# Decode attention with adaptive layernorm and token MLP: four stages as wide matmuls, and the last head with V as the stationary operand

## The chip, the cores and the metric

One core of one Trainium2 chip. The metric is the time of one execution of the whole program on the device, in microseconds; the profile's span is counted from the first to the last instruction of one profiled execution.

## The reference

One decode step of a transformer block, four batches (B), one token each, model width D = 512, everything in fp32. Six vectors of modulation come from `silu(c) @ w_mod`. Attention has 32 query heads of width 128 that share 8 K/V heads (four query heads each) over a cache of 4096 positions. The second half is the token-mixing MLP of an MLP-Mixer with a token axis of length 1: each of the 512 channels is expanded to 1792 values, passed through Gelu and contracted to one value again.

```python
mod = (silu(c) @ w_mod).reshape(B, 6, 1, -1)          # sa, ca, ga, sb, cb, gb
h = layernorm(x) * (1 + ca) + sa
q = (h @ wq).reshape(B, 1, 32, 128) ...
p = softmax(q @ k.T * 128 ** -0.5)                      # per head, k and v shared by 4 heads
x = x + ga * ((p @ v) @ wo)
h = layernorm(x) * (1 + cb) + sb
u = gelu(layernorm(h)[b, 0, d] * w1[0, f] + b1[f])      # (B, D, F), F = 1792
x = x + gb * (u @ w2 + b2)
```

## The kernel before

The work is a list of 32 heads (4 batches x 8 K/V heads; `i = b * 8 + h`). Each head brings a K tile and a V tile, 2 MB each, which go through one ring of five buffers of that size (`ring`, tag `kv`); the weights of the query projection and of the modulation use the same ring. All loads are issued on SyncE's queue in program order: in pass `i` of the main loop (L446) K of head `i + 3` and V of head `i + 1`. A K buffer comes free when the scores of its head are done, a V buffer when its values are done. The last V is cut into pieces of a half, a quarter and two eighths (L177).

The order of the instructions on every engine is the order of the program (`manual_schedule`, L42). Pass `i` holds, in this order:

- an epilogue step, if `i % 8 == 5` (L450);
- `transposes(i + 1)` (L231): eight 128x128 transposes of the exponentials `p`, the row sums `pl`, then on VectorE (DVE) the copy `pT`, the reciprocal and `sel`, which selects and scales the rows of a query head;
- `project_a(i - 1)` (L266): one matmul with the values `po` as stationary operand and `sel` as moving one, which gives the head's output transposed, `oT`;
- `scores(i + 2)` (L200): eight matmuls of 512 columns, with the four query heads in 32-column strips of the array, so that a strip `c` (partitions 32c to 32c + 31 of the result) holds a quarter of the positions; then the maximum `m` of each row;
- `project_b(i - 1)` (L274): 16 matmuls of 128 columns against `wo`, each strip `c` holding a quarter of the 512 channels, all four query heads accumulated in PSUM; then the add onto the batch's accumulator on DVE;
- `colmax(i + 2)` and `expo(i + 2)` (L211, L219): the maximum over the four strips (a transpose and a DVE reduction `mx` of 128 elements), its broadcast `pb` by four matmuls, and the exponential on ScalarE (ACT);
- an epilogue step of the batch before, if `i % 8 < 5` (L467);
- in passes 3 to 5 one modulation vector (`mod`, L193), which is computed for each batch separately, 64 matmuls in all;
- `values(i)` (L248): 32 matmuls of 128 columns. Block `k` of the positions and strip `c` choose the stationary piece of `pT` and the moving 128 positions of V; each strip accumulates over eight blocks. Then `po`, the copy out of PSUM, on DVE (L259).

PE is TensorE; an fp32 matmul appears in the profile as two, each with its own weight load (PEld).

A batch's second half runs as a generator, `epilogue` (L362), whose steps are handed out one per pass: in pass `i % 8 == 0` statistics, in 1 the layernorm, in 2 the second layernorm, the broadcast of the channels to all partitions and the first three Gelus of 1024 elements a partition (L379), in 3 the contraction of those (`contract`, L356) and two more Gelus, in 4 the same with the last two, in 5 the last contraction. For batch 2 half of this last contraction waits until the end (L386, L486). Gelu and exp need different activation tables on ACT.

For the last batch the gate `ga` is folded into `wo` of head 7 beforehand (`fold_gate`, L429, in pass 25), so that the last projection accumulates straight onto the residual in PSUM (`pgx`, L484). After the loop come `project_a`, `project_b` of head 30, the values of head 31 and its projection (L480 to L488), and `finish` (L391): the whole epilogue of batch 3 with nothing beside it but the last modulation vector (the gate `gb`), then two output DMAs.

In the kernel before, `px`, `prep`, the accumulator and everything of a batch in the second half have 128 columns with strip `c` holding channels 128c to 128c + 127, 32 equal rows in each strip.

## Time and profile before

| | |
|---|---|
| median of the runs | 396.02 us (395.72 to 396.19) |
| span of the profiled execution | 394.4 us, some 1.6 us less than the time of a run |
| TensorE | busy 73% of the span, 5414 matmuls and as many weight loads |
| DVE, ACT | busy 38% and 24% |
| DMA | 158 MB, mean 401 GB/s |
| granted TensorE clock, mean | 0.943 |

A line of a timeline gives the start and the length in us, the engine, the line of the kernel, the operation, what is written from what, the shapes, the number of instructions merged in the line, and in brackets the idle time of the engine before it with what ended it. A group's line has the busy time in us and the mean of one in ns, then the idle time before and its releasers. A window's line has, after its length, the busy time and the count on PE, PEld, DVE, ACT and POOL, then the granted clock, the share of the DMA engines and GB/s. PEld is the part of TensorE that loads the stationary operand. Matmuls are pipelined, so the mean of one is longer than the distance between two. A few records of matmuls are missing in the trace, which shows as short idle times put down to "issue".

### The profile page before, as it was taken

To read this page: it belongs to the slowest core of one execution; us is meant where nothing else is said; L and a number is where in the kernel's file an instruction comes from. 1 tells how busy PE (TensorE), PEld (TensorE's weight loads), DVE (VectorE), ACT (ScalarE), POOL (GpSimd) and SP (SyncE) were. 2 spreads that over 40 slices of the span, in tenths; PEclk is the share of its full clock that TensorE was granted. 3 is DMA by queue.
4 is the path that set the end of the run, shared out by engine and by line. 5 is a ranking of instruction groups with operands and counts; after the bars stand their busy time and mean duration, and the time that the engine had idled before them with its cause. 6 is when DMAs were issued, how large, how long until landed. Compare 5 with 4: busy or idle time off the path is not lost.

```text
span 394.4 us, 11762 instructions
## 1 busy us (share of the span) xinstructions
PE 288.9 (73%) x5414; PEld 194.4 (49%) x5414; DVE 151.4 (38%) x487; ACT 96.4 (24%) x119; POOL 0.7 (0%) x6
## 2 busy tenths in 40 slices
PE   0976785539967586778677787779776787897884
PEld 0122444408745444556455455557544464675763
DVE  4222222203222232556432334546323345763266
ACT  1001111101110111136641011348411010685125
POOL 0000000000000000000000000000000000000000
PEclk9989689959999889999999899989999898999999
DMA  8999999999999999999999999999999999999700
GB/s 321 425 430 437 431 419 433 420 430 433 429 420 432 429 429 429 427 432 429 429 421 429 430 434 429 424 425 431 432 429 427 425 429 434 427 425 417 289 8 2
DMA packets 12720, 158.08 MB, mean 401 GB/s; under 512 B 1516, under 2 KB 1532, under 8 KB 1920
## 3 DMA queue, kind: packets, MB, share of 16 engines
q1 hardware_dynamic: 12672, 157.34, 93.9%
q8 instruction: 42, 0.69, 0.6%
q14 instruction: 6, 0.05, 0.0%
HBM read 157.32 MB, written 0.01 MB: 399 GB/s over the span
## 4 chain that ended last, share of the span: by engine, by line
DMA 56%; PE 29%; DVE 8%; ACT 4%; issue 1%; SPq 0%; ACTq 0%; DVEq 0%
DMA k<-in_kT 43%; DMA v<-in_v 11%; PE s L205 10%; PE pv L254 5%; DVE m L208 3%; PE s L126 2%; PE s L235 2%; DMA sm<-in_small 2%; PE py L359 2%; DVE u L354 1%; PE pa L282 1%; ACT uu L414 1%; PE pm L190 1%; ACT p L228 1%; PE qs L141 1%
## 5 line engine op out<-in xcount | busy, mean ns | idle before, releaser
L205 PE MATMUL s<-k,QT 128*32 128x512 f32 x512 | 74.0, 703 | 40.3 <-DMA k<-in_kT 40.2
L228 ACT ACTIVATE p<-s,nm 128x1024 f32<-128x1024 f32 x32 | 35.6, 1114 | 234.5 <-DVE nm L225 234.5
L208 DVE TENSOR_REDUCE m<-s 128x1 f32<-128x1024 f32 x32 | 39.2, 1225 | 101.5 <-PE s L205 101.5
L254 PE MATMUL pv<-v,pT 128*32 128x128 f32 x2048 | 64.5, 277 | 5.6 <-DMA v<-in_v 4.5
L254 PEld LDWEIGHTS pv<-v,pT 128*32 128x32 f32 x2048 | 56.2, 111 | 7.6 <-DMA v<-in_v 5.3
L205 PEld LDWEIGHTS s<-k,QT 128*32 128x32 f32 x512 | 14.7, 119 | 66.4 <-DMA k<-in_kT 41.4
L282 PEld LDWEIGHTS pa<-wo,oT 128*32 128x32 f32 x992 | 30.2, 116 | 22.3 <-issue 21.2
L235 PE MATMUL s<-ident,p 128*128 128x128 f32 x256 | 36.4, 286 | 0.7 <-ACT p L228 0.4
L282 PE MATMUL pa<-wo,oT 128*32 128x128 f32 x992 | 34.6, 282 | 0.8 <-DVE oT L271 0.8
L235 PEld LDWEIGHTS s<-ident,p 128*128 128x128 f32 x256 | 28.6, 145 | 6.9 <-issue 6.3
L259 DVE COPY po<-pv 128x128 f32<-128x128 f32 x32 | 9.3, 290 | 41.9 <-PE pv L254 41.9
L354 DVE TENSOR_SCALAR u<-hb,wr,sm 128x512 f32<-128x512 f32 x42 | 20.0, 542 | 2.5 <-PE py L359 2.2
L214 PE MATMUL pm<-ident,m 128*1 128x128 f32 x32 | 8.7, 271 | 16.7 <-DVE m L208 16.7
L379 ACT ACTIVATE u<-u 128x1024 f32<-128x1024 f32 x21 | 20.9, 1047 | 0.1
L238 DVE COPY pT<-s 128x128 f32<-128x128 f32 x32 | 9.3, 290 | 24.8 <-PE s L235 23.6
L223 PE MATMUL pb<-neg,mx 1*32 1x1 f32 x256 | 7.6, 176 | 13.3 <-DVE mx L216 13.3
L214 PEld LDWEIGHTS pm<-ident,m 128*1 128x1 f32 x32 | 2.5, 79 | 28.8 <-DVE m L208 28.8
L126 PE MATMUL s<-wm,sT 128*4 128x512 f32 x16 | 9.6, 771 | 9.7 <-DVE sT L114 9.7
L269 PE MATMUL pt<-sel,po 128*128 128x4 f32 x64 | 11.8, 254 | 4.5 <-DVE po L259 2.9
L228 ACT ACT_TABLE_LOAD x9 | 11.5, 1283 | 13.2 <-DVE nm L225 13.1
L223 PEld LDWEIGHTS pb<-neg,mx 1*32 1x32 f32 x256 | 4.9, 103 | 19.5 <-DVE mx L216 19.5
L359 PE MATMUL py<-u,sm 128*32 128x128 f32 x336 | 11.6, 276 | 2.9 <-ACT u L379 2.9
(114 smaller groups left out, 233.1 us busy)
## 6 DMA issues: line engine op xcount, KB each, us to landing
k<-in_kT SPq DMA_DIRECT2D x32, 2048.0 KB, 22.6
v<-in_v SPq DMA_DIRECT2D x29, 2048.0 KB, 22.5
wq<-in_wq SPq DMA_DIRECT2D x4, 2048.0 KB, 18.0
wo<-in_wo SPq DMA_DIRECT2D x8, 1024.0 KB, 23.1
v<-in_v SPq DMA_DIRECT2D x5, 1024.0 KB, 19.0
wm<-in_wmod SPq DMA_DIRECT2D x2, 2048.0 KB
wm<-in_wmod SPq DMA_DIRECT2D x2, 1024.0 KB, 16.4
v<-in_v SPq DMA_DIRECT2D x1, 512.0 KB, 20.2
```

Of the source, the lines that this page charges most:

```text
L126: mm(s0[0:B, t * D:(t + 1) * D], sT[:, k, :], wm01[:, t, k, :], start=(k == 0), stop=(k == 3))
L205: mm(s[32 * c:32 * c + 32, n * 512:(n + 1) * 512], QT[:, b, h, :], KT[i][:, (n * 4 + c) * 512:(n * 4 + c + 1) * 512], start=True, stop=True)
L208: dv.tensor_reduce(m, s, axis=AX.X, op=OP.max)
L223: mm(pb[32 * c:32 * c + 32, :], mx, neg1, start=True, stop=True)
L228: nc.scalar.activation(p, s, AF.Exp, bias=nm, accum_out=l)
L235: nc.tensor.transpose(pt[:, k, :], p[:, k * P:(k + 1) * P], ident)
L254: mm(pv[32 * c:32 * c + 32, :], pTs[i % 2][:, k, c, :], VT[i][:, k * 4 + c, :], start=(k == 0), stop=(k == 7))
L269: mm(pt, po, sel, start=True, stop=True)
L282: mm(pa[32 * c:32 * c + 32, :], oT[:, g:g + 1].to_broadcast([P, 32]), wo_t[h][:, g, c * P:(c + 1) * P], start=(g == 0 and not folded), sto ...
L354: dv.tensor_scalar(u[:, e, :], hb, wr[:, j:j + 1], b1[:, j:j + 1], op0=OP.mult, op1=OP.add)
L359: mm(py[32 * c:32 * c + 32, :], w2[:, j:j + 1].to_broadcast([P, 32]), u[:, e, c * P:(c + 1) * P], start=(j == 0), stop=(j == NF - 1))
L379: nc.scalar.activation(u, u, AF.Gelu_apprx_tanh)
```

## The change

- *Values.* Eight matmuls of 512 columns instead of 32 of 128: all 16 used columns of a block (four strips of four query heads) against four neighbouring pieces of V at once. A strip now holds two of the eight blocks, and of the 16 x 512 results in it only the matching quarters are wanted. The copy `po` is four times as wide and moves from DVE to ACT.
- *Project_a.* Four matmuls, accumulated, each with a 128x128 piece of `po` as stationary operand; `sel` (16 columns) picks the wanted quarter.
- *Project_b.* Four matmuls of 512 columns, strip `g` holding query head `g`; the accumulator is 128x512. The four rows are summed once for a batch (`fold_groups`) by four matmuls, before the residual.
- *Modulation and `px`.* All four batches at once: the 32 columns of a strip are four batches of eight rows (`sT8`, `rows`). So `prep` has no batch axis; the rows of batch `b` start at `32 c + 8 b`.
- *Contraction of batches 0 to 2.* Column block `j` of the MLP goes whole (512 columns) into strip `j % 4`; a copy `yw` and `fold_groups` follow. The step in which the last blocks are contracted is pass `i % 8 == 5`, for batch 2 too, and one more step follows in pass 6. The contraction of batch 3 stays narrow.
- *Maximum.* `mx` is written four times over by one reduction that reads its input four times, and `pb` is one matmul.
- *The last batch.* The gate is folded into `wo` of heads 6 and 7 (passes 25 and 26); heads 30 and 31 are projected straight onto the residual. Head 31 has V as the stationary operand: 32 matmuls of four columns, whose result is the transposed output, scaled in one multiply; no `po` and no `project_a`.
- *Output.* One DMA for each batch, that of batch 2 on ACT's queue, instead of one for batches 0 to 2 and one for batch 3.

```diff
-    def modmm(pm, t, steps):
-        for b, k in steps:
+    def modmm(pm, t):
+        for k in range(4):
             for c in range(4):
-                mm(pm[32 * c:32 * c + 32, b, :], sT[:, k, b:b + 1].to_broadcast([P, 32]),
+                mm(pm[32 * c:32 * c + 32, :], sT8[:, k].rearrange("p b r -> p (b r)"),
                    WM[t][:, k, c * P:(c + 1) * P], start=(k == 0), stop=(k == 3))
...
-        dv.tensor_reduce(mx, pm.rearrange("o (c r) -> o r c", c=4), axis=AX.X, op=OP.max)
+        dv.tensor_reduce(mx, pm.rearrange("o (c r) -> o r c", c=4).unsqueeze(1).to_broadcast([1, 4, 32, 4]),
+                         axis=AX.X, op=OP.max)
...
-        for c in range(4):
-            mm(pb[32 * c:32 * c + 32, :], mx, neg1, start=True, stop=True)
+        mm(pb, mx.rearrange("o c r -> o (c r)"), neg1, start=True, stop=True)
...
+    def values(i):
+        pv = ps_v.tile([P, 4 * DH], F32, name="pv")
+        for k in range(8):
+            q = k % 4
+            mm(pv[32 * q:32 * q + 32, :], pTs[i % 2][:, k, :],
+               VT[i][:, k * 4:(k + 1) * 4, :].rearrange("p j d -> p (j d)"), start=(k < 4), stop=(k >= 4))
+        po = wk.tile([P, 4 * DH], F32, name="po")
+        nc.scalar.activation(po, pv, AF.Copy)
+        SP[i] = (SEL.pop(i), po)
...
+    def values_last(i, js):
+        if js[0] == 0:
+            PV[i] = ps_v.tile([P, REP], F32, name="pvT", tag="pv")
+        for j in js:
+            k, c = divmod(j, 4)
+            mm(PV[i], VT[i][:, j, :], pTs[i % 2][:, k, c * REP:(c + 1) * REP], start=(j == 0), stop=(j == 31))
+        if js[-1] == 31:
+            oT = wk.tile([P, REP], F32, name="oT")
+            dv.tensor_mul(oT, PV.pop(i), SEL.pop(i))
+            OT[i] = oT
...
-        mm(pt, po, sel, start=True, stop=True)
+        for c in range(4):
+            mm(pt, po[:, c * DH:(c + 1) * DH], sel[:, c * REP:(c + 1) * REP], start=(c == 0), stop=(c == 3))
...
+        pa = ps_m.tile([P, D], F32, name="pa", tag="m")
+        for g in range(REP):
+            mm(pa[32 * g:32 * g + 32, :], oT[:, g:g + 1].to_broadcast([P, 32]), wo_t[h][:, g, :],
+               start=True, stop=True)
+        if h == 0:
+            ACC[b] = wk.tile([P, D], F32, name="acc")
+            dv.tensor_copy(ACC[b], pa)
+        else:
+            dv.tensor_add(ACC[b], ACC[b], pa)
...
+    def fold_groups(pool, acc, tag):
+        pc = pool.tile([P, P], F32, name="pc", tag=tag)
+        for c in range(4):
+            mm(pc[32 * c:32 * c + 32, :], first, acc[:, c * P:(c + 1) * P], start=True, stop=True)
+        return pc
...
+    def contract_wide(py, u, js):
+        for e, j in enumerate(js):
+            q = j % 4
+            mm(py[32 * q:32 * q + 32, :], w2[:, j:j + 1].to_broadcast([P, 32]), u[:, e, :],
+               start=(j < 4), stop=(j >= NF - 4))
...
         for u, js in done:
-            contract(py, u, js)
-            if b == B - 2:
-                yield
-        dv.tensor_scalar(ZK[:, b], py, b2, None, op0=OP.add)
+            contract_wide(py, u, js)
+        yw = wk.tile([P, D], F32, name="yw", bufs=1)
+        dv.tensor_copy(yw, py)
+        yield
+        dv.tensor_scalar(ZK[:, b], fold_groups(ps_e, yw, "e"), b2, None, op0=OP.add)
         yield
...
-        if i % HKV == 5:
+        if i % HKV >= 5:
             next(epi, None)
...
-        values(i, range(8))
-        if i == NS - HKV + 1:
-            fold_gate()
+        values(i)
+        if NS - HKV < i <= NS - HKV + 2:
+            fold_gate(HKV - 3 + i - (NS - HKV))
+    residual(ep, fold_groups(ps_e, ACC.pop(B - 1), "e"))
+    pgx = ps_s.tile([P, 8, P], F32, name="pgx", tag="s")
+    x3 = pgx[:, 4]
     project_a(NS - 2)
-    project_b(NS - 2)
-    values(NS - 1, (0, 1, 2, 3, 4, 5))
-    pgx = ps_s.tile([P, 8, P], F32, name="pgx", tag="s")
-    mm(pgx[:, 4], ident, EP.pop(B - 1), start=True, stop=False)
-    values(NS - 1, (6, 7))
-    next(epi)
-    project_a(NS - 1)
-    project_b(NS - 1, pgx[:, 4])
-    finish(B - 1, pgx, pgx[:, 4], epi)
+    mm(x3, ident, ep, start=True, stop=False)
+    project_direct(NS - 2, x3, False)
+    values_last(NS - 1, range(0, 28))
+    values_last(NS - 1, range(28, 32))
+    project_direct(NS - 1, x3, True)
+    finish(B - 1, pgx[:, 0], x3, epi)
```

`project_direct` issues the 16 narrow matmuls that `project_b` issued before, onto `x3`.

More of the change, by code (lines that the diff above doesn't have):

```diff
@@ L335, in bcast @@
         for c in range(4):
-            mm(pb[:, c, :], ident[:, 32 * c:32 * c + 1].to_broadcast([P, P]), h1, start=True, stop=True)
+            e = 32 * c + 8 * b
+            mm(pb[:, c, :], ident[:, e:e + 1].to_broadcast([P, P]), h1, start=True, stop=True)
         return pb.rearrange("p c n -> p (c n)")
@@ L393, in finish @@
         U = [uu[j // 8][:, j % 8] for j in range(NF)]
-        stm = stats(xp)
+        stm = stats(xp, b)
         dv.tensor_copy(XK[:, b], xp)
-        gate = [divmod(e, 4) for e in range(4 * B)]
         pst = gather(stm)
-        modmm(pg, 5, gate[:6])
+        modmm(pg, 5)
         h1, stm = adaln(b, pst)
@@ L445, in adaln_decode @@
     epi = iter(())
+    ep = cst.tile([P, P], F32, name="ep")
     for i in range(NS - 1):
```

143 lines of the change are left out of this document (62 added, 81 removed).

## The prediction

> **What bounds the kernel now.** I read the slices of the span first, then the busy time by windows, then the groups of instructions, and last the timeline of one ordinary pass of the main loop, of the three passes in which the token MLP of batch 2 is worked off, and of the end.
>
> ```profile
> DMA  8999999999999999999999999999999999999700
> ```
> ```profile
> 200.00:240.00 40.00, 30.41 (x556) 20.40 (x558) 13.24 (x46) 5.28 (x9) 0.00 (x0) 0.96 1.01 428
> 374.50:375.00 0.50, 0.50 (x23) 0.50 (x27) 0.00 (x0) 0.00 (x0) 0.00 (x0) 1.00 0.60 229
> ```
>
> The transfers fill the span up to about 375 us. One pass brings one K and one V, 4.194 MB, which at 428 GB/s is 9.80 us: a pass whose instructions take less waits for DMA, a pass that takes more falls behind, and the passes after it may catch up. What is behind when the last V has landed is paid in full, and so is everything after it. The question is therefore what the change does to the length of a pass, and to the end.
>
> **The wide matmuls.** Groups of instructions (count, busy us, mean ns of one):
>
> ```profile
> L205 PE MATMUL s<-k,QT 128*32 128x512 f32 x512 | 74.0, 703 | 40.3 <-DMA k<-in_kT 40.2
> L254 PE MATMUL pv<-v,pT 128*32 128x128 f32 x2048 | 64.5, 277 | 5.6 <-DMA v<-in_v 4.5 <-issue 0.9
> L208 DVE TENSOR_REDUCE m<-s 128x1 f32<-128x1024 f32 x32 | 39.2, 1225 | 101.5 <-PE s L205 101.5
> L216 DVE TENSOR_REDUCE mx<-pm 1x32 f32<-1x128 f32 x32 | 8.9, 277 | 4.6 <-PE pm L214 4.6
> L290 DVE TENSOR_TENSOR acc<-acc,pa 128x128 f32<-128x128 f32 x24 | 6.7, 279 | 3.2 <-PE pa L282 3.2
> L435 DVE TENSOR_TENSOR wo<-wo,pgb 128x512 f32<-128x512 f32 x4 | 2.5, 682 | 0.3 <-PE pgb L432 0.3
> L347 ACT ACTIVATE hb<-phb,nmean 128x512 f32<-128x512 f32 x3 | 2.1, 687 | 0.5 <-PE phb L336 0.2
> ```
>
> And an ordinary pass in order of time (start us, us), the last two lines from another pass:
>
> ```profile
> 314.31 1.95 PE L254 MATMUL pv<-v,pT 128*32 128x128 f32 x64
> 316.20 0.86 PEld L235 LDWEIGHTS s<-ident,p 128*128 128x128 f32 x8 [0.20 <-issue]
> 317.02 0.30 PEld L237 LDWEIGHTS pl<-l,grp 128*128 128x128 f32 x2
> 317.24 0.30 PEld L269 LDWEIGHTS pt<-sel,po 128*128 128x128 f32 x2
> 318.17 1.92 PE L205 MATMUL s<-k,QT 128*32 128x512 f32 x16 [0.53 <-DMA k<-in_kT]
> 320.16 1.23 DVE L208 TENSOR_REDUCE m<-s 128x1 f32<-128x1024 f32 x1 [2.06 <-PE s L205]
> 321.44 0.27 PE L214 MATMUL pm<-ident,m 128*1 128x128 f32 x1 [0.48 <-DVE m L208]
> 321.75 0.28 DVE L216 TENSOR_REDUCE mx<-pm 1x32 f32<-1x128 f32 x1 [0.17 <-PE pm L214]
> 322.08 0.24 PE L223 MATMUL pb<-neg,mx 1*32 1x1 f32 x8 [0.37 <-DVE mx L216]
> 323.03 1.95 PE L254 MATMUL pv<-v,pT 128*32 128x128 f32 x64
> 349.05 0.30 PEld L269 LDWEIGHTS pt<-sel,po 128*128 128x128 f32 x2
> 349.37 1.92 PE L205 MATMUL s<-k,QT 128*32 128x512 f32 x16
> ```
>
> 64 narrow matmuls of `pv` take 1.95 us; 16 matmuls of scores, with the shape and the four column strips that the wide values will have, take 1.92 us. Both stream 8192 columns. Values and projection thus lose three quarters of their instructions and no time; I cost them at nothing. The modulations really do a quarter of the work, but in passes 3 to 5, under DMA: nothing. The narrow contraction also streams equally; wide, though, a pair of columns of the MLP uses two of four strips, so it takes two rounds of 0.43 to 0.48 us (a quarter of 1.92) where the narrow pair took about 0.45.
>
> The Trainium skill, TensorE: Matmul & The Clock Gate, section Back-to-back issue gap, gives about 81 ns for each matmul of 128 columns and 131 ns for 512, a gain of 3 us a head by instruction count alone; the rows (1.95 us for 64, 1.92 us for 16) say otherwise, and the sum goes by the rows.
>
> **What a pass gets longer by.** *Project_a* goes from one matmul to four, each of two passes with a 128-column weight load: six loads more. Two such loads separate 317.02 from 317.24, 0.11 us each: +0.66. *The row maximum* is now reduced from 512 elements: between 277 ns for 128 and 1225 ns for 1024, in proportion 0.68 us: +0.41. *The accumulator add* is 128x512 from PSUM: 682 ns (L435) in place of 279. It stands on DVE ahead of the row maximum, which started 1.59 us after `m` (321.75 less 320.16) and now starts after 1.23 + 0.69 + gaps of 0.06: +0.39. Fewer `pb` matmuls save under 0.1, which I leave. Sum +1.46.
>
> The ordinary pass, without its DMA wait: values to transposes 1.89, to `pl` 0.82, to `pt` 0.22, to scores 0.32 (349.05 to 349.37), to `m` 1.99, to `pm` 1.28, to `mx` 0.31, to `pb` 0.33, to the values about 0.2: 7.36 us. After: 8.82, still below 9.80. It catches up 1.0 us a pass instead of 2.4.
>
> **The copy that moves to ACT.** The evacuation of the values, 0.29 us on DVE, becomes a 128x512 copy on ACT, 0.69 us (687 ns, L347). In an ordinary pass ACT is free then. In the three passes of an epilogue that start the Gelus, the copy stands behind them in ACT's program; `project_a` waits for it, and the next scores stand behind `project_a` on PE.
>
> ```profile
> 328.73 0.36 PE L269 MATMUL pt<-sel,po 128*128 128x4 f32 x2 [1.67 <-DVE wo L435]
> 329.21 3.48 PE L205 MATMUL s<-k,QT 128*32 128x512 f32 x16
> 338.61 2.95 ACT L379 ACTIVATE u<-u 128x1024 f32<-128x1024 f32 x3
> 340.08 0.28 DVE L259 COPY po<-pv 128x128 f32<-128x128 f32 x1
> 340.41 0.39 PE L269 MATMUL pt<-sel,po 128*128 128x4 f32 x2 [0.82 <-DVE po L259]
> 340.73 1.92 PE L205 MATMUL s<-k,QT 128*32 128x512 f32 x16
> 345.19 1.28 ACT L228 ACT_TABLE_LOAD   x1 [3.62 <-DVE nm L225]
> 349.00 2.00 ACT L379 ACTIVATE u<-u 128x1024 f32<-128x1024 f32 x2
> 351.02 1.28 ACT L228 ACT_TABLE_LOAD   x1
> 356.30 2.00 ACT L379 ACTIVATE u<-u 128x1024 f32<-128x1024 f32 x2
> 359.35 1.92 PE L205 MATMUL s<-k,QT 128*32 128x512 f32 x16
> ```
>
> The copy already waits behind DVE's expansion once, and `pt` behind it (0.82 us). Behind the Gelus it is worse. I take it that a copy needs no activation table of its own (`hb`, of the same kind, runs between exp and Gelu, and the tables loaded are those two); else each would add 1.28. From scores to scores:
> - first pass: 329.21 to the end of three Gelus at 341.56, less 1.56 for scores at half clock (3.48 against 1.92), is 10.79; +0.80 for add and maximum, +0.74 copy, +0.98 for `pt` (0.32 + 0.66): 13.3.
> - second: 340.73 to 351.00, less the load of the exp table of 1.28 that was not hidden here (at 351.02 it was), 8.99; the same additions: 11.5.
> - third: 349.37 to 358.30, 8.93, +0.80. Now both pairs are contracted ahead of the transposes, so the second Gelu is waited for: +0.9 wide pair, 0.82, 0.22, 0.98: 12.6.
>
> Together 37.4 us against 29.4 of DMA: each of the three epilogues falls 8.0 us behind. The five passes between take 44.1, plus 0.3 for folding the four row groups and 0.75 for the statistics step (`pb` to values 0.95 at 322.08, not 0.2): 45.2 against 49.0, 3.8 us back. Behind, in turn: 8.0, 4.2, 12.2, 8.4. The first of the two gate foldings (there was one) makes DVE hold `pt`, 1.67 us in the row, less 0.28 for the copy that has left DVE: 9.8. After the third epilogue 17.8. Now it is 30.14 less 29.4, 0.7. Scores of the last head come **17.1 us later**. DMA doesn't starve: five buffers hold 24 us of transfers, and the landings stay ahead of PE. If the copy's cover were complete, see the second rival.
>
> **The end.**
>
> ```profile
> 358.57 0.33 SPq L179 DMA_DIRECT2D v<-in_v  x1
> 372.04 2.02 PE L254 MATMUL pv<-v,pT 128*32 128x128 f32 x48
> 377.26 0.30 DVE L307 BATCH_NORM_STATS2 st<-pgx 128x6 f32<-128x128 f32 x1 [1.20 <-PE pgx L282]
> 381.16 0.97 PEld L336 LDWEIGHTS py<-h,ident 128*128 128x128 f32 x8
> 391.79 0.55 SPq L427 DMA_DIRECT2D out<-osb  x1
> ```
> ```profile
> DMA to landing us min/median/max: 14.7/18.9/20.2
> ```
>
> From the last scores (359.35) to the statistics (377.26) it is 17.9 us now. Added: add and maximum 0.8; `project_a` of head 29 0.66; fold of batch 2's output 0.25; for head 30 a longer copy, six loads and the identity matmul, 1.1. The last head's values, with V stationary, are 64 weight loads of 128 columns. Eight take 0.97 us in the row of L336, 0.11 each: 7.04, +0.4 for drain and the multiply, 7.45 us. From 372.04 to the projection at 376.11 (377.26 less the 1.15 us from its start to the statistics) it took 4.07, copy and `project_a` included: +3.4. Sum **+6.2**. After that the chain is the one of now, bound by DVE and Gelus. The quarter-size gate matmuls lie in gaps of PE already, and the small copies added at the start beside the first loads. Three output DMAs instead of one are issued before the last (391.79); two on SP and one on ACT behind the last Gelu fit ahead of it, else 0.6 each.
>
> The sum: span 394.4, time 396.0 (1.6 around it, and the median of the runs is 396.02): 396.0 + 17.1 + 6.2 = **419**.
>
> **Rivals.** *DMA hides the passes* and only the end is paid: 396.0 + 6.2 = 402. For it: 40.2 us of waits for K in the first row of groups. Against: the scores at 340.73, 349.37 and 359.35 show no such wait. Chance 0.12.
>
> *The copies don't queue.* Then PE alone sets the passes: 9.96 + 1.46, 8.64 + 1.46, and 9.98 + 1.46 + 0.9 for the second Gelu, 33.9: 4.5 behind each time, 3.8 back, some 6.5 at the last scores, less 0.6 at the end: 396.0 + 6.5 + 5.6 = 408. The Trainium skill, TensorEngine Tiling (Array Packing), section PSUM Bottleneck, asks to use ScalarE beside VectorE for emptying PSUM, which would be this case; the row at 349.00 shows ACT taken at just that place. Chance 0.14.
>
> *Faster.* Without `po` and `project_a` of the last head little follows the last V. Its last quarter of a buffer lands at 373.3 (358.57 + 14.7, the youngest in that row); four chunks 0.88, drain and multiply 0.4, projection 1.15: statistics at 375.7 instead of 377.26, 394.4 in all. It decides if PE has the other 56 loads (6.2 us) behind it by 373.3, that is starts them by 367.1; now it gets there at 372.04. It takes matmuls bound by issue, not by columns. Chance 0.07. *No change* within 0.2% (about what a measurement tells apart): gain and loss cancel, 0.05.
>
> **The numbers.** Forecast 419, chance 0.62. Above it: the exp table's load unhidden once in each epilogue, 3.8; three scores at half clock, 1.56 each, 4.7: 428. Below, the range takes in both slower rivals: 402. Left out are 0.12 below and some 0.06 above. Faster 0.07, same 0.05, slower 0.88.
>
> **What would show it.** Right: 16 wide matmuls of values at 1.9 us; the copy on ACT starting at the end of the Gelus in passes 10 to 12, 18 to 20, 26 to 28, with `pt` waiting for ACT; scores intervals near 13, 11.5 and 12.6 us there and 8.8 elsewhere late; DMA share falling in the last quarter; about 7 us for the last values. Wrong: waits of the scores for K right up to head 31, or last values under 3 us.

## The result, and the profile after

The changed kernel takes **437.84 us** (median of 4, 436.96 to 438.74) against 396.01 before: ratio **1.1056 (1.1037 to 1.1075)**. The profiled span is 435.1 us (before 394.4), the mean granted clock 0.886 (0.943). Three points split the 40.7 us that the span grew: the maximum of head 31 (right behind its scores) starts 28.1 us later, the stretch from there to the statistics is 11.3 us longer (27.25 against 15.92), the finish 1.3 (18.41 against 17.14).

The slices of the page of after: clock, DMA share and GB/s.

```profile
PEclk9988698689698889898999988979999988899558
DMA  8999999999999999999999999988999997850000
GB/s 335 428 422 432 429 425 415 435 425 419 431 424 425 428 429 425 429 425 428 425 429 428 426 428 425 426 310 309 420 425 428 426 402 295 287 196 2 2 0 2
```

The transfers now run below their full rate at 283 to 305 us and from 350 us on (before, the slices of DMA were full up to the last three), and the clock halves where the last head is computed. Groups of instructions of after (count, busy us, mean ns of one):

```profile
L209 PE MATMUL s<-k,QT 128*32 128x512 f32 x512 | 76.3, 722 | 19.5 <-DMA k<-in_kT 19.5
L260 PE MATMUL pv<-v,pT 128*32 128x512 f32 x496 | 67.0, 642 | 0.1
L286 PE MATMUL pt<-sel,po 128*128 128x4 f32 x248 | 32.7, 255 | 13.0 <-ACT po L263 9.7
L220 DVE TENSOR_REDUCE mx<-pm 1x128 f32<-1x512 f32 x32 | 21.5, 672 | 1.1 <-PE pm L218 1.1
L302 DVE TENSOR_TENSOR acc<-acc,pa 128x512 f32<-128x512 f32 x26 | 17.7, 680 | 3.5 <-PE pa L296 3.4
L263 ACT ACTIVATE po<-pv 128x512 f32<-128x512 f32 x31 | 18.4, 592 | 21.9 <-PE pv L260 21.9
```

The scores wait 19.5 us for K instead of 40.3, none of it after 150 us: from there PE, not DMA, sets the passes. 496 wide matmuls of values are busy 67.0 us; before, 2048 narrow ones, with one head more, 64.5. An ordinary pass of after (timeline):

```profile
306.81 1.92 PE L209 MATMUL s<-k,QT 128*32 128x512 f32 x16
309.95 0.68 DVE L302 TENSOR_TENSOR acc<-acc,pa 128x512 f32<-128x512 f32 x1
310.54 0.67 DVE L220 TENSOR_REDUCE mx<-pm 1x128 f32<-1x512 f32 x1
311.27 0.38 PE L227 MATMUL pb<-neg,mx 1*128 1x1 f32 x2 [0.91 <-DVE mx L220]
311.58 1.92 PE L260 MATMUL pv<-v,pT 128*32 128x512 f32 x16
314.50 1.03 PE L286 MATMUL pt<-sel,po 128*128 128x4 f32 x8
315.47 1.07 PE L209 MATMUL s<-k,QT 128*32 128x512 f32 x8
```

From scores to scores it is 8.66 us (forecast 8.82); of the scores in the last line the window shows the first half. The three passes of batch 1's MLP:

```profile
265.53 2.95 ACT L407 ACTIVATE u<-u 128x1024 f32<-128x1024 f32 x3
268.39 0.57 ACT L263 ACTIVATE po<-pv 128x512 f32<-128x512 f32 x1
269.01 1.06 PE L286 MATMUL pt<-sel,po 128*128 128x4 f32 x8 [1.92 <-ACT po L263]
270.00 1.92 PE L209 MATMUL s<-k,QT 128*32 128x512 f32 x16
275.10 1.28 ACT L232 ACT_TABLE_LOAD   x1 [6.14 <-DVE nm L229]
280.82 0.58 ACT L263 ACTIVATE po<-pv 128x512 f32<-128x512 f32 x1
281.45 1.61 PE L286 MATMUL pt<-sel,po 128*128 128x4 f32 x8 [1.93 <-ACT po L263]
283.00 3.64 PE L209 MATMUL s<-k,QT 128*32 128x512 f32 x16
297.94 1.92 PE L209 MATMUL s<-k,QT 128*32 128x512 f32 x16
```

The copy starts when the last Gelu ends, and PE waits 1.9 us for it. After the first such wait the scores still take 1.92 us; after the second they run at half clock, 3.64 us. The exp table's load at 275.10 stands open in front of the exponential. The end, and its windows (busy PE, PEld, DVE, ACT, POOL, clock, DMA share, GB/s):

```profile
402.53 11.91 PE L273 MATMUL pvT<-pT,v 128*128 128x4 f32 x64
414.69 1.94 PE L309 MATMUL pgx<-wo,oT 128*32 128x128 f32 x32 [0.26 <-DVE oT L276]
416.69 0.30 DVE L327 BATCH_NORM_STATS2 st<-pgx 128x6 f32<-128x128 f32 x1 [2.06 <-PE pgx L309]
```
```profile
403.00:406.00 3.00, 3.00 (x24) 3.00 (x23) 0.00 (x0) 0.00 (x0) 0.00 (x0) 0.77 0.02 5
406.00:409.00 3.00, 3.00 (x16) 3.00 (x16) 0.00 (x0) 0.00 (x0) 0.00 (x0) 0.50 0.00 0
```

PE is busy without a gap, and its clock halves all the same: 24 loads fit into the first 3 us, 16 into the next.

### The profile page after: what moved, and what is told of

Same layout as the page of the kernel before. It is cut to its first block, busy times and chain, and to the rows that moved or that the text cites. A ratio compares the mean times of both kernels' runs of the same rounds, so it can differ in the third digit from the quotient of the medians.

```text
span 435.1 us, 6196 instructions
## 1 busy us (share of the span) xinstructions
PE 332.2 (76%) x2602; PEld 160.7 (37%) x2602; DVE 169.9 (39%) x459; ACT 113.8 (26%) x150; POOL 0.7 (0%) x6
## 4 chain that ended last, share of the span: by engine, by line
PE 54%; DMA 18%; DVE 17%; ACT 8%; issue 2%; SPq 0%; ACTq 0%
DMA k<-in_kT 16%; PE s L209 15%; PE pv L260 9%; DVE m L212 6%; PE pt L286 5%; PE s L239 4%; DVE mx L220 4%; DVE acc L302 3%; ACT u L407 3%; PE pvT L273 3%; PE pa L296 2%; PE pb L227 2%; PE s L129 2%; PE py L386 2%; PE qs L144 2%
## 5 line engine op out<-in xcount | busy, mean ns | idle before, releaser
L209 PE MATMUL s<-k,QT 128*32 128x512 f32 x512 | 76.3, 722 | 19.5 <-DMA k<-in_kT 19.5
L260 PE MATMUL pv<-v,pT 128*32 128x512 f32 x496 | 67.0, 642 | 0.1
L286 PE MATMUL pt<-sel,po 128*128 128x4 f32 x248 | 32.7, 255 | 13.0 <-ACT po L263 9.7
L239 PEld LDWEIGHTS s<-ident,p 128*128 128x128 f32 x256 | 28.5, 144 | 23.9 <-ACT p L232 13.1
L296 PE MATMUL pa<-wo,oT 128*32 128x512 f32 x240 | 36.8, 689 | 0.3 <-DVE oT L288 0.3
L286 PEld LDWEIGHTS pt<-sel,po 128*128 128x128 f32 x248 | 30.7, 195 | 13.8 <-ACT po L263 12.1
L227 PE MATMUL pb<-neg,mx 1*128 1x1 f32 x64 | 12.1, 256 | 30.5 <-DVE mx L220 30.5
L209 PEld LDWEIGHTS s<-k,QT 128*32 128x32 f32 x512 | 14.8, 120 | 44.9 <-issue 24.3
L260 PEld LDWEIGHTS pv<-v,pT 128*32 128x32 f32 x496 | 15.2, 115 | 26.6 <-issue 26.0
L263 ACT ACTIVATE po<-pv 128x512 f32<-128x512 f32 x31 | 18.4, 592 | 21.9 <-PE pv L260 21.9
L220 DVE TENSOR_REDUCE mx<-pm 1x128 f32<-1x512 f32 x32 | 21.5, 672 | 1.1 <-PE pm L218 1.1
L302 DVE TENSOR_TENSOR acc<-acc,pa 128x512 f32<-128x512 f32 x26 | 17.7, 680 | 3.5 <-PE pa L296 3.4
L386 PE MATMUL py<-u,sm 128*32 128x512 f32 x84 | 14.9, 602 | 3.4 <-ACT u L407 3.4
## 6 DMA issues: line engine op xcount, KB each, us to landing
v<-in_v SPq DMA_DIRECT2D x29, 2048.0 KB, 17.6
```

What stands on the lines that cost most here:

```text
L209: mm(s[32 * c:32 * c + 32, n * 512:(n + 1) * 512], QT[:, b, h, :], KT[i][:, (n * 4 + c) * 512:(n * 4 + c + 1) * 512], start=True, stop=True)
L220: dv.tensor_reduce(mx, pm.rearrange("o (c r) -> o r c", c=4).unsqueeze(1).to_broadcast([1, 4, 32, 4]), axis=AX.X, op=OP.max)
L227: mm(pb, mx.rearrange("o c r -> o (c r)"), neg1, start=True, stop=True)
L239: nc.tensor.transpose(pt[:, k, :], p[:, k * P:(k + 1) * P], ident)
L260: mm(pv[32 * q:32 * q + 32, :], pTs[i % 2][:, k, :], VT[i][:, k * 4:(k + 1) * 4, :].rearrange("p j d -> p (j d)"), start=(k < 4), stop=(k ...
L286: mm(pt, po[:, c * DH:(c + 1) * DH], sel[:, c * REP:(c + 1) * REP], start=(c == 0), stop=(c == 3))
```

## The experiments

"Late" is how much later than in the kernel before the maximum of head 31 starts, "end" the time from there to the statistics, "finish" the rest of the span; all from the profiles. A profile is one execution, whose time can lie at an end of the range: at the upper one for `four_256`, `six_256` and `before_later`, at the lower one for after, `copy_dve`, `exp_pre`, `warm` and `three` among others.

| kernel | us (range) | ratio (interval) | late | end | finish |
|---|---|---|---|---|---|
| before | 396.0 | 1 | 0 | 15.9 | 17.1 |
| after | 437.84 (436.96 to 438.74) | 1.1056 (1.1037 to 1.1075) | 28.1 | 27.3 | 18.4 |
| last_plain | 428.09 (426.09 to 428.74) | 1.0795 (1.0763 to 1.0827) | 28.5 | 18.2 | 18.5 |
| last_stream | 432.82 (431.75 to 433.55) | 1.0925 (1.0903 to 1.0947) | 28.9 | 21.9 | 18.4 |
| copy_dve | 426.35 (424.33 to 428.29) | 1.0763 (1.072 to 1.0807) | 14.8 | 27.6 | 18.8 |
| max_narrow | 424.77 (424.36 to 426.32) | 1.0731 (1.0709 to 1.0753) | 16.5 | 26.3 | 18.5 |
| exp_pre | 436.14 (434.09 to 437.16) | 1.0999 (1.0965 to 1.1034) | 26.1 | 26.4 | 18.5 |
| warm | 430.37 (429.59 to 435.65) | 1.0905 (1.0832 to 1.0977) | 19.5 | 28.6 | 18.5 |
| three | 409.54 (406.86 to 409.73) | 1.0319 (1.0285 to 1.0353) | 7.8 | 17.7 | 18.3 |
| three_gate | 408.84 (406.78 to 412.53) | 1.0335 (1.0288 to 1.0383) | 7.6 | 17.7 | 18.4 |
| four | 402.33 (401.46 to 403.17) | 1.016 (1.0141 to 1.018) | 5.5 | 15.5 | 17.3 |
| four_256 | 400.54 (399.89 to 403.49) | 1.0118 (1.0077 to 1.0158) | 6.6 | 15.5 | 18.2 |
| five_256 | 401.75 (399.53 to 402.26) | 1.0121 (1.0082 to 1.016) | 4.9 | 15.3 | 18.2 |
| one_fold_256 | 398.08 (397.75 to 401.58) | 1.0067 (1.0041 to 1.0093) | 1.1 | 15.7 | 18.2 |
| six_256 | 397.33 (396.31 to 398.48) | 1.0026 (1.0017 to 1.0035) | 1.5 | 15.6 | 18.2 |
| after_256 | 436.57 (434.55 to 436.89) | 1.1002 (1.0971 to 1.1032) | 28.0 | 27.1 | 18.5 |
| before_vstat | 410.59 (410.22 to 411.7) | 1.0366 (1.0347 to 1.0384) | 3.2 | 25.4 | 18.8 |
| before_pad | 399.60 (399.23 to 399.94) | 1.0091 (1.0078 to 1.0105) | 3.3 | 16.3 | 17.1 |
| before_512 | 396.21 (395.78 to 397.0) | 0.9996 (0.9984 to 1.0007) | 0.3 | 15.8 | 17.2 |
| before_later | 397.76 (397.26 to 399.03) | 1.0042 (1.0028 to 1.0055) | -0.7 | 18.2 | 18.5 |

**The last head.** `last_plain` computes it like the others, `last_stream` gives each of V's weight loads 64 moving columns instead of 4, `before_vstat` puts V stationary into the kernel before.

```diff
-    values_last(NS - 1, range(0, 28))          # last_plain
-    values_last(NS - 1, range(28, 32))
+    values(NS - 1)
+    project_a(NS - 1)
...
-            mm(PV[i], VT[i][:, j, :], pTs[i % 2][:, k, c * REP:(c + 1) * REP], start=(j == 0), stop=(j == 31))
+            mm(PV[i].rearrange("p a r -> p (a r)"), VT[i][:, j, :],     # last_stream
+               pTs[i % 2][:, k, c * REP:(c + 1) * REP].unsqueeze(1).to_broadcast([P, 16, REP]),
+               start=(j == 0), stop=(j == 31))
...
-    values(NS - 1, (0, 1, 2, 3, 4, 5))         # before_vstat, with the change's values_last
+    values_last(NS - 1, range(0, 24))
...
-    values(NS - 1, (6, 7))
+    values_last(NS - 1, range(24, 32))
...
-    project_a(NS - 1)
```

> The changed kernel (437.8 us), with the last head done like the others: wide values, copy on ACT, project_a, then the projection onto the residual. Theory A, V as the stationary operand costs the end in two ways, 64 weight loads and a TensorE clock that falls to half (0.50 granted from 406 to 427 us) and stays there through the finish: 11.9 us of loads give way to 1.9 + 0.65 + 0.95, 8.4 us; the last projection takes 1.1 instead of 2.0 and the finish 17.1 instead of 18.4: 10.6 less, about 427 us, clock 1.0 at the end. Rival: the clock falls at the end for another reason (nothing else runs beside), then only the loads at their full-clock price go, about 5 us less, 433 us, and the finish stays at half clock.

> The changed kernel, V stationary for the last head as it is, but with 64 moving columns in each matmul (the four columns repeated 16 times, only the first four used). At full clock a weight load of 128 columns takes 0.11 us and hides them. Theory A1, the granted clock follows the columns that are streamed, and four for each load are too few: the clock stays at 1.0, the 64 loads take about 7.1 us instead of 11.9, projection and finish 2.2 less, about 431 us. Rival A2, the clock falls because of the weight loads or the operand pattern whatever is streamed: no change, 437 to 438 us, clock 0.5.

> The kernel before (396.0 us) with one part of the change alone: the last head with V as the stationary operand, 32 matmuls of four columns, no copy and no project_a for it. Theory A, the clock falls after about 2 us of such matmuls, as in the changed kernel: 11.9 + 0.4 us take the place of 4.1, then the last projection at half clock 0.9 more and the finish up to 1.3 more: 405 to 406.5 us. Rival A0, the clock in the changed kernel falls for what surrounds them there: the loads take 7.0, 3.4 us more in all, 399.4 us.

Without V stationary 9.8 us are gone; in the profiles it is the end alone that gets shorter (by 9.1 us). With 16 times as many columns the same 64 loads are faster. The groups of `last_stream` and of after:

```profile
L273 PEld LDWEIGHTS pvT<-pT,v 128*128 128x128 f32 x64 | 7.2, 192 | 0.2 <-issue 0.2
```
```profile
L273 PEld LDWEIGHTS pvT<-pT,v 128*128 128x128 f32 x64 | 11.8, 291 | 0.2 <-issue 0.2
```

And the timeline of `last_stream`:

```profile
403.28 7.36 PE L273 MATMUL pvT<-pT,v 128*128 128x64 f32 x64
410.89 1.08 PE L311 MATMUL pgx<-wo,oT 128*32 128x128 f32 x32 [0.25 <-DVE oT L278]
```

The clock stays at 1.00 there up to 416 us, and the projection behind takes 1.08 us instead of 1.94. So the shape as such takes 7.4 us, as the forecast had it, and the end is 21.9 us, close to the 15.9 of before and the 6.2 added by the forecast. The rest is the clock: PE is busy without a gap in both runs, and they differ in the columns that stream behind each load. In `before_vstat` the end grows by 9.4 us and the finish by 1.7; that it is also 3.2 late has another cause (the offset, below). With it the time lies above both its forecasts. The finish keeps its 18.4 to 18.5 us in `last_plain` and `last_stream`, so V as the stationary operand is not what lengthens it.

**The late passes.** One part undone each: the copy of the values on DVE, the maximum of 128 elements with four `pb` matmuls, both with `last_plain` (`three`); the exp table loaded early; and eight idle matmuls where PE waits for the copy.

```diff
-        nc.scalar.activation(po, pv, AF.Copy)                # copy_dve
+        dv.tensor_copy(po, pv)
...
-        mx = wk.tile([1, 4, 32], F32, name="mx")             # max_narrow
-        dv.tensor_reduce(mx, pm.rearrange("o (c r) -> o r c", c=4).unsqueeze(1).to_broadcast([1, 4, 32, 4]),
-                         axis=AX.X, op=OP.max)
+        mx = wk.tile([1, 32], F32, name="mx")
+        dv.tensor_reduce(mx, pm.rearrange("o (c r) -> o r c", c=4), axis=AX.X, op=OP.max)
...
+        if i >= HKV and i % HKV == 2:                        # exp_pre, behind the copy
+            nc.scalar.preload_act_table(AF.Exp)
...
-        pt = ps_m.tile([P, REP], F32, name="pt", tag="m")    # warm, in project_a
+        pw = ps_m.tile([P, D], F32, name="pt", tag="m")
+        pt = pw[:, 0:REP]
+        if i >= HKV and 2 <= i % HKV <= 3:
+            for e in range(8):
+                mm(pw[:, P:2 * P], ident, ident, start=True, stop=True)
```

> The changed kernel with the 128x512 copy of the values on DVE (0.69 us) instead of ACT. Theory Q, the copy queued behind the Gelus is the larger part of what the passes lost (28 us at the scores of the last head): the three epilogues fall behind by 4 to 5 us each instead of 10 to 13, and 3 to 4 of that is caught up between them; 16 to 21 us less, 417 to 422 us, and the last V is waited for nearly without lag. Rival P, every pass is longer by 1.5 us and the clock is lower, and the queue matters little: under 6 us less, 432 us or more.

> The changed kernel with the row maximum as before: a reduction of 128 elements (0.28 us in place of 0.67) and four small matmuls for its broadcast. Theory P, from head 10 on the passes run behind the DMA, so that each microsecond in the chain from scores to values is paid in the end: 21 passes at 0.4 us, 8 to 9 us less, about 429 us. Rival: the chain is set by ACT in the epilogue passes and by DMA elsewhere, then under 3 us, 435 us or more.

> The changed kernel with three parts undone at once: last head like the others, copy of the values on DVE, narrow row maximum. What stays of the change: wide values, wide projection and its accumulator, project_a in four matmuls, wide contraction, modulations for all batches at once. One by one the three gave 9.8, 11.5 and 13.1 us less. Theory S, they pay in different places (the end, ACT's queue in the epilogue passes, the chain of every pass), so that they add up: about 403 to 405 us. Rival: copy and maximum shorten the same waits, and the last one alone is worth little beside the first: 410 us or more.

> The changed kernel with the exp table loaded on ACT right after the copy of the values in the first pass of each epilogue, instead of when the maximum is there. In the changed kernel this load stood after the wait for the maximum, in the way of exp, in the second pass of each epilogue (three times 1.28 us). If ACT's chain sets those passes: 3 to 4 us less, 434 us. Rival: PE sets them, and nothing changes (437 to 438).

> The changed kernel with eight idle matmuls (identity times identity, 1.7 us at full clock, into an unused part of a PSUM tile) ahead of project_a in the two passes of each epilogue in which PE waits there some 1.9 us for the copy. Nothing of the result changes. Theory C, PE's idle time in these passes takes its clock to half, and the scores, projections and values after it pay (scores 3.6 instead of 1.9 us): with PE busy the clock stays, 3 to 8 us less, 430 to 435 us. Rival: the clock falls for other reasons, and the extra matmuls cost up to 0.3 us in each of six passes: 438 to 440.

`copy_dve` gives 11.5 us back, between the two theories: PE still waits for the copy in the first of the three passes (0.25 us in batch 0, 1.25 in batch 1), but no longer for the Gelus. `max_narrow` gives 13.1, more than expected: an ordinary pass is 8.1 us and not 8.66, and from head 13 on each such 0.55 counts, 18 times. That is 9.9 of the 11.6 us by which its last scores come earlier; the rest is not accounted for. The parts alone add up to 34.3 us; together they give 28.3, since with less lateness DMA sets the pace again (`three` is at most 0.3 us late at heads 26 to 28). `exp_pre` gives 1.7 and not 3.8: the second passes get shorter by 0.6 to 1.0 us, not by 1.28. `warm` confirms the clock: 48 matmuls that compute nothing (96 in the profile) make the kernel 7.5 us faster. Timeline of `warm`, the second and third of these passes:

```profile
266.35 1.92 PE L209 MATMUL s<-k,QT 128*32 128x512 f32 x16
275.74 2.03 PE L288 MATMUL pt<-ident 128*128 128x128 f32 x16
277.18 0.58 ACT L263 ACTIVATE po<-pv 128x512 f32<-128x512 f32 x1
278.79 1.92 PE L209 MATMUL s<-k,QT 128*32 128x512 f32 x16
```

The scores there take 1.92 us, where the third pass of after had 3.64. The waits for the copy are not the only places where the clock falls, though. The values of the pass ahead of these three in after, and the window behind their start:

```profile
250.58 3.24 PE L260 MATMUL pv<-v,pT 128*32 128x512 f32 x16
252.00:255.00 3.00, 3.00 (x20) 1.33 (x13) 1.15 (x5) 0.60 (x1) 0.00 (x0) 0.59 1.01 431
```

They take 3.24 us instead of 1.92, though the longest wait of PE in the 5 us before them is 0.91 us.

**What is left.** `four`: also `values`, its copy (128x128) and `project_a` (one matmul) as before. `five_256`: also `contract` as before. `one_fold_256`: the gate is folded into head 31's weights alone. `six_256`: also `project_b` as before; only the quarter-size modulations stay. `three_gate` is `three` with the gate modulation issued four times. The ones with 256 have an unused tile, below. Apart from the lines here, the edits are the lines of the change's diff, taken back.

```diff
-                py = ps_e.tile([P, D], F32, name="py", tag="e")   # five_256, with contract for contract_wide
+                py = ps_e.tile([P, P], F32, name="py", tag="e")
...
-        yw = wk.tile([P, D], F32, name="yw", bufs=1)
-        dv.tensor_copy(yw, py)
         yield
-        dv.tensor_scalar(ZK[:, b], fold_groups(ps_e, yw, "e"), b2, None, op0=OP.add)
+        dv.tensor_scalar(ZK[:, b], py, b2, None, op0=OP.add)
...
-        residual(XK[:, b], fold_groups(ps_e, ACC.pop(b), "e"))   # six_256, with project_b of before
+        residual(XK[:, b], ACC.pop(b))
...
         modmm(pg, 5)                                         # three_gate, in finish
+        modmm(pg, 5)
...
-        if NS - HKV < i <= NS - HKV + 2:                     # one_fold_256
-            fold_gate(HKV - 3 + i - (NS - HKV))
+        if i == NS - HKV + 1:
+            fold_gate(HKV - 1)
-    residual(ep, fold_groups(ps_e, ACC.pop(B - 1), "e"))
...
     project_a(NS - 2)
-    mm(x3, ident, ep, start=True, stop=False)
-    project_direct(NS - 2, x3, False)
+    project_b(NS - 2)
     values(NS - 1)
+    residual(ep, fold_groups(ps_e, ACC.pop(B - 1), "e"))
+    mm(x3, ident, ep, start=True, stop=False)
```

> The kernel with the three parts undone, and in addition values and project_a narrow as before the change (one matmul in project_a in place of four, a 128x128 copy in place of 128x512). What stays of the change: the wide projection with its 128x512 accumulator, the wide contraction, the quarter-size modulations. Theory L: the six more weight loads of project_a (0.66 us) and the longer copy (0.4 us) lengthen the late passes by 1.0 us; the 7.8 us by which the last scores were still late with the three parts undone fall to 1 to 4, and the time is 401 to 405. Rival: what is still late comes from the accumulator's add and the two folds; the last scores stay 6 us or more late and the time is 407.5 or more.

> The last one, and the wide contraction of the token MLP undone too (of batches 0 to 2; a pair of columns needs one round of four strips again, and no fold and no copy of its output stand on DVE). What stays of the change is the wide projection with its 128x512 accumulator, its fold, and the quarter-size modulations. Theory: the wide contraction is what holds the third pass of each epilogue, 0.5 to 0.9 us each, and the fold of its output; 1.5 to 3 us less than the last one, 397.3 to 398.8. Rival: the accumulator's add and its fold are what is left; under 0.8 us less.

> The kernel with everything undone but wide projection and quarter-size modulations, ring at the offset of the kernel before; now the gate is folded into the weights of head 31 alone, as before the change, and head 30 goes through the accumulator. If the second folding is the cause, the last scores come 2 to 3 us earlier (1.7 us that the projection waited for one folding, and the rest of its four multiplies) and the time is 398.5 to 400. Rival, the accumulator's add: no change within 0.8 of 401.7; the time may also rise by up to 0.6, the projection of head 30 onto the end.

> The same, and the projection narrow again with its 128x128 accumulator. What stays of the change is the quarter-size modulations alone. Theory: nothing is left that lengthens a pass; the last scores within 0.5 us of the kernel before, and 395.5 to 396.5. Rival: the quarter-size gate matmuls take work from TensorE at the end and let its clock fall, 397 to 398; a gain, under 395.4, is the other way.

> The kernel with the three parts undone (copy on DVE, narrow maximum, last head as the others), and in the finish the quarter-size gate modulation issued four times instead of once, so that TensorE streams as many columns there as before the change; the output is the same. Theory C: from the statistics of the last head to the end of the span it took 18.3 us in place of 17.1 because the removed gate matmuls no longer keep the clock up; with them back the finish takes 17.1 to 17.4 again and the time is about 408.4, 1.1 less than with the three parts undone. Rival: the clock falls there for another reason; the finish stays at 18.2 or more and the time at 409.5 or above.

`four` is 7.2 us faster than `three`; in the profiles, which are 5.5 us apart, 2.3 of it are in the passes, 2.2 at the end and 1.0 in the finish. The 1.0 can't be credited to the parts undone: `four_256`, the same program with an unused tile, has the longer finish again. The wide contraction is no cause that these runs resolve: `five_256` is 1.2 us above `four_256`, with intervals that overlap. The second folding is one: 3.7 us by the medians, with ranges that overlap by one execution of each, and 3.8 us at the last scores in the profiles. It falls into the pass of the three Gelus of the last batch but one. `five_256` and `one_fold_256` there:

```profile
340.11 2.47 DVE L459 TENSOR_TENSOR wo<-wo,pgb 128x512 f32<-128x512 f32 x4
342.72 0.36 PE L287 MATMUL pt<-sel,po 128*128 128x4 f32 x2 [2.36 <-DVE wo L459]
343.01 3.20 PE L211 MATMUL s<-k,QT 128*32 128x512 f32 x16
```
```profile
339.69 0.36 PE L287 MATMUL pt<-sel,po 128*128 128x4 f32 x2
339.98 1.92 PE L211 MATMUL s<-k,QT 128*32 128x512 f32 x16
```

PE waits 2.36 us for four multiplies, and the scores after the wait take 3.20 us. `one_fold_256` also moves the projection of head 30, so the 3.7 us are those of both. The narrow projection gives another 0.75 (a difference that the ranges don't separate), and 1.3 us are left in `six_256`; its profile, of an execution of 398.48, the longest of eleven, has the last scores 1.5 late and the finish 1.1 longer. `three_gate` did not shorten the finish, so the gate matmuls that were taken away are not the cause by themselves; `before_later` has all of them and 18.5. Nearly the whole difference lies between the statistics and the first multiply of the MLP's expansion. The windows from the one to the other in `before`, `four`, `four_256` and `six_256`:

```profile
377.26:383.26 6.00, 4.75 (x101) 4.19 (x104) 4.46 (x24) 0.86 (x2) 0.00 (x0) 1.00 0.01 3
382.32:388.32 6.00, 3.39 (x48) 2.75 (x48) 4.46 (x24) 0.86 (x2) 0.00 (x0) 0.95 0.01 3
383.46:390.40 6.94, 5.40 (x48) 4.46 (x48) 4.46 (x23) 0.69 (x2) 0.00 (x0) 0.58 0.01 2
378.37:385.31 6.94, 5.47 (x48) 4.52 (x48) 4.46 (x23) 0.69 (x1) 0.00 (x0) 0.58 0.00 0
```

It is 6.0 us at a clock of 0.95 or 1.00 and 6.7 to 7.7 us at a lower one, in all twenty kernels. `four` and `four_256` issue the same instructions there.

**The offset.** `before_pad`, `before_512` and `after_256` only add an unused tile of 16, 256 and 352 bytes a partition behind the constants, which moves the ring of K and V (by 32 bytes for 16).

```diff
+    pad = cst.tile([P, 64], F32, name="pad")                 # before_512; 88 in after_256, 96 in four_256
+    dv.memset(pad, 0.0)
```

> The kernel before with nothing changed but one small tile more in on-chip memory, which is written once and never read; it shifts the addresses of the tiles behind it. The kernel before with V stationary in its last head, which has such a tile too, had its transfers at 424 GB/s in place of 428 and its last scores 3.2 us later. Theory M: the place in memory sets the rate; here too 424 GB/s and about 399. Rival: it does not; 396.0 within 0.4 and 428 GB/s.

> The kernel before, with an unused tile of 256 bytes a partition behind its constants, so that its ring of five K and V buffers, which lies 256 bytes past a multiple of 512, lies on one. Theory M1 (what counts is a multiple of 64 or 128 bytes, which 256 keeps and the 32 of the earlier run broke): 428 GB/s and 396.0. Theory M2 (the nearer to a multiple of 512 the better): more than 430 GB/s and under 395. Theory M3 (it is not the offset but something else that an added tile changes): 424 GB/s and 399.5.

> The changed kernel with an unused tile of 352 bytes a partition behind its constants, so that its ring lies 256 bytes past a multiple of 512, as in the kernel before, in place of 416. If the offset is a term of the loss, the passes that wait for K get 428 GB/s in place of 426, the last scores come 1 to 2.5 us earlier, and the time is 435.3 to 436.8. Rival: in the late passes PE sets the pace and the rate is hidden; 437.8 within 0.6.

> The kernel with the three parts and project_a undone, with 384 bytes more behind its constants: ring at the offset of the kernel before. If the offset is a term: 428 GB/s in place of 425 to 427, the last scores 2 us earlier, about 400.3. Rival: 402.3 within 0.5.

The windows from 120 to 200 us of `before`, `before_pad`, `before_512`, `after`, `after_256`, `four` and `four_256`, in this order:

```profile
120.00:200.00 80.00, 57.00 (x1120) 40.57 (x1110) 31.81 (x105) 23.32 (x28) 0.00 (x0) 0.96 1.01 428
```
```profile
120.00:200.00 80.00, 60.68 (x1181) 42.21 (x1175) 31.73 (x103) 20.58 (x27) 0.00 (x0) 0.89 1.01 425
```
```profile
120.00:200.00 80.00, 58.11 (x1127) 41.34 (x1123) 31.90 (x104) 22.63 (x28) 0.00 (x0) 0.94 1.01 429
```
```profile
120.00:200.00 80.00, 62.59 (x493) 29.18 (x492) 31.40 (x89) 23.17 (x31) 0.00 (x0) 0.89 1.01 426
```
```profile
120.00:200.00 80.00, 63.78 (x479) 29.30 (x468) 31.70 (x88) 22.89 (x31) 0.00 (x0) 0.87 1.01 430
```
```profile
120.00:200.00 80.00, 59.18 (x897) 33.63 (x887) 33.81 (x103) 24.06 (x30) 0.00 (x0) 0.91 1.01 425
```
```profile
120.00:200.00 80.00, 61.94 (x884) 35.13 (x877) 34.30 (x104) 24.28 (x30) 0.00 (x0) 0.89 1.01 429
```

The ring starts 0, 32, 0, 160, 0, 128 and 0 bytes past a multiple of 256, and the rate goes with it: 428 to 430 GB/s on one, 425 to 426 beside (`three`, 128 bytes past, has 427). `before_512` takes as long as before although it has an added tile too, so it is the offset that counts. In a kernel that DMA bounds it costs 3.6 us (`before_pad`), but the median of `after_256` is only 1.3 below that of after, and its profile as late at head 31: PE's late passes hide the rate. `four_256` is 1.8 us below `four`, with intervals that overlap and a profile in which the last scores come 1.1 us later, so no gain is shown there. The Trainium skill, DMA: Bandwidth & Descriptors, section How a descriptor splits into AXI transactions, has the first piece of a descriptor that does not start at a multiple of 256 bytes begin at the multiple below, and fetch bytes that are not used. The page tells it of reads; these rows show a lower rate by the place that is written, and no run shows whether the reason is the same.

**A faster version.** `before_later` moves two steps of the MLP in the kernel before: that of pass `i % 8 == 5` behind the exponential of its pass, and the last one of batch 2 ahead of the projection of head 30:

```diff
-        if i % HKV == 5:
-            next(epi, None)
...
-        if i % HKV < 5:
+        if i % HKV <= 5:
...
+    next(epi)
     project_a(NS - 2)
...
-    next(epi)
     project_a(NS - 1)
```

> A version meant to beat both: the kernel before with the last step of the token MLP of each batch moved, within pass 5 of eight, behind the exp of that pass, and the last step of batch 2 ahead of the projection of head 30, so that the last scores are not held by the 0.7 us by which they were late; the output is the same. Theory: 0.6 to 1.2 less, 394.8 to 395.4. Rival: that time is hidden or given back at the end; 396.0 within 0.4.

It takes 397.76 us instead of 396.0: in its profile (the longest of five executions, 399.03) the last scores come 0.7 us earlier, but the stretch behind them is 2.2 us longer and the finish runs at half clock from 380 to 386 us. No version beats the kernel before.

## Why the forecast was right or wrong

The forecast was 419 us, with a range of 402 to 428. By the profiles, 11.0 of the 18.8 us above it are later scores of the last head, 5.1 the end and 1.3 the finish. The mechanism was right, and three of its terms were too small: the three passes of the MLP (37.4 us), the gate folding (one of two) and the weight loads of the last head ("0.11 each").

- *The sign, and that both passes and end are paid*: right. DMA did not hide the passes (402) and the copies do queue (408 did not come).
- *Wide matmuls at no gain*: right, 1.92 us for 16 as for 64 narrow ones (1.95). The figures of the Trainium skill, TensorE: Matmul & The Clock Gate, section Back-to-back issue gap, by which they would gain, do not hold for these shapes.
- *A pass longer by 1.46*: right in its terms (`project_a` 1.03 against 0.36, maximum 0.67, add 0.68), but `pb` costs 0.14 more (0.38 against 0.24) where it was to save under 0.1: one load of 128 columns stands for four of 32.
- *The copy behind the Gelus*: right, and shown by `copy_dve`, 11.5 us. The copy itself takes 0.59 us on ACT, not 0.69.
- *The three passes, 37.4 us*: too small; they took 39.9, 41.8 and 42.5 (scores to scores from 170.26 to 210.20, 256.11 to 297.94, 344.96 to 387.45). Two subtractions failed. "Less the load of the exp table of 1.28 that was not hidden here": it is open in the second pass now too (275.10), where moving it ahead (`exp_pre`) saves 0.6 to 1.0 us. "Less 1.56 for scores at half clock": the wait for the copy replaces the wait for DVE, and the scores behind it fall to a lower clock, in the third pass (3.38, 3.64 and 3.16 us), and behind the wait for the second folding too (2.94). With the clock kept up (`warm`) the second and third passes of all three batches take 12.4 and 12.6 to 12.7 us; the forecast had 11.5 and 12.6. Both stood in the upper end of the range, as risks; they were the rule.
- *The gate folding, +1.4*: it priced the first of two. The second costs some 3.7 us.
- *Scores of the last head 17.1 late*: 28.1. After the three epilogues (heads 15, 23 and 31) they are 8.6, 17.6 and 28.1 late, where the forecast had 8.0, 12.2 and 17.1. Between the first two only 1.2 us were caught up instead of 3.8: the kernel before took 47.1 us there and not 49.0, and the values at 250.58 ran at a low clock.
- *V stationary, 7.45 us*: 11.9, and the projection behind it 1.94 instead of 1.08. With `last_stream`'s 7.4 and 1.08 the end is as forecast, so this is the whole of the 5.1 by which the end (+11.3 against +6.2) was too small. The step that failed is "0.11 each": measured on a run of eight loads with 128 moving columns, it held for 64 loads with 64 columns each (7.2 us); with four columns each the clock fell after some 2 us, and the 64 took 11.8.
- *The finish is the chain of now*: 1.3 longer, because the steps between the statistics and the MLP's expansion ran at half clock (7.2 us instead of 6.0). What makes the clock fall there is open: the finish takes 17.1 to 17.3 us in four of these kernels and 18.2 to 18.8 in the others, `before_later` among them, and `four` and `four_256` differ in it with the same instructions.
- *DMA doesn't starve*: right for PE (no scores wait for K after 150 us). DMA itself idles, since the late scores give the buffers back late.
- *The offset of the ring* was in no term: 426 for 428 GB/s, some 1.3 us here.

By undoing part after part the 41.8 us are: copy, maximum and V stationary 28.3; `project_a` with the wide copy 7.2; the offset 1.8; wide contraction none that shows (-1.2); second folding 3.7; wide projection 0.75; modulation with the finish's clock 1.3. The last five are differences whose ranges overlap or that hang on the clock of the finish; only that of the second folding is borne out by a wait in the profile.

## What to carry to other kernels

Fewer, wider instructions gained nothing here, where the columns stayed the same, and what they add around them (loads, wider copies, wider reductions) is paid in every pass once the passes are longer than their transfers. Price a wait on PE with the clock that it takes from the work behind it, and price a stream of weight loads by columns streamed, not by PE's being busy. Before a copy moves to a free engine, look at what that engine does in its worst pass, not in its mean one. (The copy on ACT ahead of the Gelus was not tried.)

## What the runs showed of the hardware

- TensorE's clock halved while PE was busy 3.00 of 3.00 us, on 128-column loads with 4 moving columns each (11.8 us for 64); with 64 columns each it stayed at 1.00 (7.2 us). The Trainium skill, TensorE: Matmul & The Clock Gate, section What's actually happening, has the clock go by how busy the PE has recently been; the rows agree only if a load with little behind it does not count as busy, and the measurement decides.
- A wait of 1.9 us, shorter than the window of about 3.4 us that the same section names, stood ahead of scores at half clock (3.64 us at 283.00). The first of two such waits did not do it (1.92 us at 270.00), and the values at 250.58 lost their clock (0.59) with no wait above 0.91 us, so the length of one wait does not decide. Idle matmuls in the waits kept the scores at 1.92 us in all three epilogues.
- The rate of transfers was 428 to 430 GB/s where the buffers start at a multiple of 256 bytes and 425 to 427 where they do not, enough to hide or feign an effect of 3.6 us: an added tile of 16 bytes cost as much as the second folding.
